# Memory rows by DMA, a shorter keep-warm block and another order of the first seven tiles in an attention, SoLU and top-1 MoE kernel

## Chip, cores and metric

The kernel runs on one core of a Trainium2 chip. The metric is device time in microseconds of the whole program, start to end. Lower is better.

## What is computed

Three layers follow each other on 3,072 tokens (4 batches of 768) with 512 features. Cut to what matters:

```python
# attention: 8 heads of 64, chunks of 32 queries; each sees 8 memory keys and the keys 16 before to 8 after its chunk
for c in range(24):
    k_full = concat([mem_k, k[:, :, max(0, 32*c - 16):min(768, 32*c + 40)]])
    v_full = concat([mem_v, v[:, :, max(0, 32*c - 16):min(768, 32*c + 40)]])
    out[:, :, 32*c:32*c + 32] = softmax(q_c @ k_full.T / 8) @ v_full
x = out as (3072, 512)
# SoLU layer, 512 -> 1024 -> 512
h = x @ w_in
s = h * softmax(h)
x = ((s - mean(s)) / sqrt(var(s) + 1e-6) * g_ln) @ w_out
# top-1 mixture of 8 experts, 512 -> 1024 -> 512
e = argmax(x @ w_gate)
out = softmax(x @ w_gate)[e] * sigmoid((x @ w_output_gate)[e]) * (relu(x @ w1[e]) @ w2[e])
```

`w_in`, `w_out` and `g_ln` reach the program as 64-bit floats (w_in and w_out in 32-bit halves); a float32 is made of each value on VectorE.

## The kernel before

The tokens are cut into 24 tiles of 128. Each tile goes through attention (scores, row maximum, exponentials, normalisation, transpose, product with v), then through the SoLU layer (first product, its row maximum, exponentials, squares, normalisation, transpose by DMA, second product) and the routing. After that the experts run over gathered rows. Products with the layers' weights are done in float16 in three passes, with a high and a low half of each operand.

Every step of a tile is registered with `at(t, fn)`, where t is a time of a schedule. At the end the steps are sorted by t and emitted in that order. So t only sets the order in which each engine's instructions, and the DMA issues on SyncE, stand in their queues; each queue runs in order and waits for data and for free buffers. From tile 7 on a tile has a fixed pattern with a period of 14.2 us of the schedule. The first seven tiles, all loads of that time and the conversion of the weights have their times written out by hand in the dictionary `PLAN`. `STEADY` is the place in that list that is set equal to five periods of the pattern: `when(name)` returns `PLAN[name] - STEADY + 5 * PERIOD`. In the list `w0` to `w3` load the four blocks of w_in and `w4` to `w7` those of w_out, and `b1`, `b2`, `b3`, `hi` and `lo` unpack them and make their halves. `k`, `q` and `v` load operands (k and q for two tiles each, v for one), `win` and `mkc` build the keys of a tile from its k and the memory keys, `sc` to `xlo` are the attention, `pin` and `hm` to `lt` the SoLU layer, `po` and `x2` its second product, `lg` to `rk` the routing.

`VW[0]` and `VW[1]` are two buffers with the values of two tiles each: eight chunks of 32 queries, on partitions 8 to 63 and 72 to 127 the 56 rows of v, on partitions 0 to 7 and 64 to 71 the eight memory rows, repeated for each chunk. For the first two pairs of tiles `first_mv` loads the memory rows once (two DMAs of 8 KB), and `copy_mv` repeats them into the buffers, by ScalarE for `VW[0]` and by VectorE for `VW[1]`. Later pairs use `load_mv`, in which a DMA reads the rows once for each chunk. The weight blocks have four buffers for eight loads, q and k two each; a load that takes a buffer again waits on SyncE for its last reader.

`WARM` lists blocks of matmuls on a constant tile, each of 384 columns, whose result nothing reads. An entry is its time in the list, the number of matmuls and the PSUM tile they write. The first block stands ahead of all other work of TensorE.

## Time and profile before

| | |
|---|---|
| median of 3 runs | 636.5 us (636.02 to 636.7) |
| the profiled execution | 635.88 us, span from first to last instruction 634.2 us |
| granted TensorE clock, mean of the span | 0.995 |
| TensorE matmul busy | 611.4 us (96%) |
| VectorE busy | 407.1 us (64%) |
| ScalarE busy | 311.1 us (49%) |
| GpSimd busy | 175.9 us (28%) |

The profile is of one execution. Busy time is a union of an engine's instructions and says nothing on which of them others wait for; keep-warm matmuls count as busy. Times in rows are microseconds from the span's start. The operations on w_in and w_out appear under the tile names `wd` (as loaded), `da` (as unpacked), `win_hl` and `wout_hl` (their halves).

### The profile page before, as it was taken

To read this page: it belongs to the slowest core of one execution; us is meant where nothing else is said; L and a number is where in the kernel's file an instruction comes from. 1 tells how busy PE (TensorE), PEld (TensorE's weight loads), DVE (VectorE), ACT (ScalarE), POOL (GpSimd) and SP (SyncE) were. 2 spreads that over 40 slices of the span, in tenths; PEclk is the share of its full clock that TensorE was granted. 3 is DMA by queue.
4 is the path that set the end of the run, shared out by engine and by line. 5 is a ranking of instruction groups with operands and counts; after the bars stand their busy time and mean duration, and the time that the engine had idled before them with its cause. 6 is when DMAs were issued, how large, how long until landed. Compare 5 with 4: busy or idle time off the path is not lost.

```text
span 634.2 us, 17086 instructions
## 1 busy us (share of the span) xinstructions
PE 611.4 (96%) x6955; PEld 338.3 (53%) x6955; DVE 407.1 (64%) x1209; ACT 311.1 (49%) x648; POOL 175.9 (28%) x201
## 2 busy tenths in 40 slices
PE   9999899999999999999999999999999999999993
PEld 5555445555555545545554455554554656657561
DVE  3999865878888788887876674566062537365020
ACT  5677864555665556645444242464152526444120
POOL 2213342334322343323333016030121312313101
PEclk9999999999999999999999999999999999999998
DMA  8985879699999999986459368997566485793101
GB/s 262 344 259 117 182 181 175 163 181 206 259 204 219 197 204 221 199 157 123 101 109 196 89 189 246 245 337 239 192 169 224 93 315 157 252 215 99 37 8 41
DMA packets 168262, 117.44 MB, mean 185 GB/s; under 512 B 125724, under 2 KB 149678, under 8 KB 167664
## 3 DMA queue, kind: packets, MB, share of 16 engines
q1 hardware_dynamic: 162096, 96.94, 66.1%
q0 software_dynamic: 6080, 19.34, 9.7%
q8 instruction: 56, 0.92, 0.7%
q14 instruction: 30, 0.25, 0.1%
HBM read 73.69 MB, written 12.94 MB: 137 GB/s over the span
## 4 chain that ended last, share of the span: by engine, by line
PE 37%; issue 25%; DVE 18%; POOL 6%; ACT 6%; DMA 4%; SPq 2%; POOLq 0%; ACTq 0%; DVEq 0%
PE h L582 11%; PE pt L350 8%; PE pg L350 5%; PE pt L1276 5%; DMA out_dram<-eh,split 3%; POOL out_dram L1334 3%; PE warm L909 3%; DVE nm L592 2%; ACT eh L600 2%; POOL xg L1238 2%; PE sc L367 2%; DVE eh L604 2%; DVE mx L381 1%; PE xo L458 1%; DVE e L385 1%
## 5 line engine op out<-in xcount | busy, mean ns | idle before, releaser
L582 PE MATMUL h<-win_hl,xT 128*128 128x512 f16 x576 | 131.7, 379 | 2.9 <-DVE eh L604 1.4
L350 PE MATMUL pt<-wout_hl,lnT 128*128 128x512 f16 x552 | 129.2, 379 | 1.2 <-DVE x L186 1.1
L1276 PEld LDWEIGHTS <-ru 128*128 128x128 f16 (+2 forms) x1176 | 70.1, 100 | 63.7 <-issue 5.6
L1262 DVE SCALAR_TENSOR_TENSOR ru<-pg,ru 128x320 f16<-128x320 f32 (+5 forms) x72 | 37.6, 525 | 102.6 <-ACT ru L1261 102.2
L582 PEld LDWEIGHTS <-xT 128*128 128x128 f16 x576 | 53.1, 98 | 63.7 <-issue 2.5
L350 PEld LDWEIGHTS <-lnT 128*128 128x128 f16 x576 | 53.2, 97 | 57.4 <-issue 1.5
L350 PE MATMUL pg<-xu,hl 128*128 128x320 f16 (+2 forms) x480 | 73.4, 312 | 0.7 <-ACT junk L621 0.6
L1261 ACT ACTIVATE ru<-pg 128x320 f16<-128x320 f32 (+5 forms) x72 | 33.5, 466 | 81.9 <-PE pg L350 80.0
L1276 PE MATMUL pt<-hl,ru 128*128 128x512 f16 (+2 forms) x528 | 72.8, 321 | 0.0
L648 POOL TENSOR_TENSOR lnhl<-eh,lnhl 128x1024 f16<-128x1024 f32 x23 | 49.5, 2152 | 77.7 <-ACT lnhl L644 64.6
L1276 PE MATMUL pt<-wout_hl,ru 128*32 128x128 f16 (+2 forms) x648 | 60.7, 285 | 1.2 <-issue 0.9
L350 PE MATMUL pg<-xu,win_hl 128*128 128x480 f16 (+3 forms) x384 | 59.5, 316 | 0.0
L350 PEld LDWEIGHTS <-hl 128*128 128x128 f16 x480 | 46.1, 98 | 25.0 <-DMA xu<-xg 0.7
L1334 POOL DMA_INDIRECT out_dram<-eh,slots_sidx x17 | 17.5, 1027 | 146.4 <-ACT eh L1333 146.4
L350 PEld LDWEIGHTS <-win_hl 128*128 128x128 f16 x384 | 37.2, 98 | 21.5 <-issue 0.8
L600 ACT ACTIVATE eh<-h,nm 128x1024 f32<-128x1024 f32 x24 | 26.8, 1115 | 41.8 <-DVE zr L793 34.8
L419 POOL TENSOR_TENSOR e<-e,sm 128x512 f32<-128x512 f32 x24 | 28.7, 1197 | 62.1 <-DVE sm L416 45.0
L186 DVE SCALAR_TENSOR_TENSOR hl<-wf,hl 128x1024 f16<-128x1024 f32 x32 | 38.7, 1224 | 11.0 <-ACT hl L1225 10.5
L1225 ACT ACTIVATE hl<-wf 128x1024 f16<-128x1024 f32 x32 | 32.9, 1047 | 4.2 <-DMA wf<-in_moe_w_dram 4.2
L604 DVE SCALAR_TENSOR_TENSOR eh<-h,eh 128x1024 f32<-128x1024 f32 x24 | 29.4, 1223 | 6.3 <-ACT eh L600 6.3
L909 PE MATMUL warm<-wide 128*128 128x384 f16 x169 | 31.6, 346 | 1.4 <-DVE mhalf L156 1.4
L621 ACT ACTIVATE junk<-eh,su 128x1024 f16<-128x1024 f32 x24 | 27.7, 1153 | 8.7 <-DVE pr L616 6.9
(193 smaller groups left out, 833.2 us busy)
## 6 DMA issues: line engine op xcount, KB each, us to landing
wf<-in_moe_w_dram SPq DMA_DIRECT2D x14, 2048.0 KB
vw<-in_v_dram SPq DMA_DIRECT2D x96, 112.0 KB
kr<-in_k_dram SPq DMA_DIRECT2D x12, 560.0 KB
qt<-in_q_dram SPq DMA_DIRECT2D x12, 512.0 KB
x2d<-x POOLq DMA_DIRECT2D x23, 260.0 KB
wd<-in_moe_w_in_dram SPq DMA_DIRECT2D x4, 1024.0 KB
wd<-in_moe_w_out_dram SPq DMA_DIRECT2D x4, 1024.0 KB
wf<-in_moe_w_dram SPq DMA_DIRECT2D x8, 512.0 KB
```

What stands on the lines that cost most here:

```text
L186: nc.vector.scalar_tensor_tensor(out=lo, in0=src, scalar=s, in1=hi, op0=ALU.mult, op1=ALU.subtract)
L350: nc.tensor.matmul(out=out_ap, lhsT=a, rhs=b_, start=(z == 0), stop=(z == n - 1))
L582: nc.tensor.matmul(out=v["h"][:, n * HALF:(n + 1) * HALF], lhsT=xt[:, a * KD + kk], rhs=win_hl[:, b_, kk, n * HALF:(n + 1) * HALF], start= ...
L600: nc.scalar.activation(out=v["e"], in_=v["h"], func=AF.Exp, bias=v["nm"], scale=IH, accum_out=v["se"])
L604: nc.vector.scalar_tensor_tensor(out=e, in0=v["h"], scalar=IH, in1=e, op0=ALU.mult, op1=ALU.mult, accum_out=v["su"])
L648: eng.tensor_tensor(out=v["ln"][:, 1], in0=v["e"], in1=v["ln"][:, 0], op=ALU.subtract)
L909: nc.tensor.matmul(out=t[:, 0:3 * P], lhsT=wide[:, 0:P], rhs=wide, start=True, stop=True)
L1225: nc.scalar.activation(out=hl[b, m][:, 0, cs], in_=wf[m if of is None else of][:, cs], func=AF.Copy, scale=(S_W1, S_W2)[m])
L1261: nc.scalar.activation(out=r[:, 0, f, 0:cap(n)], in_=ps, func=AF.Relu)
L1262: nc.vector.scalar_tensor_tensor(out=r[:, 1, f, 0:cap(n)], in0=ps, scalar=0.0, in1=r[:, 0, f, 0:cap(n)], op0=ALU.max, op1=ALU.subtract)
L1276: nc.tensor.matmul(out=y_t[n, piece][q * m:(q + 1) * m, 0:DM // fold], lhsT=r[:, a, kk, at_:at_ + m], rhs=wt[:, b_, kk, q * DM // fold:(q ...
L1334: put = nc.gpsimd.indirect_dma_start(out=out if fold == 1 else out.rearrange("n (h d) -> (n h) d", h=fold), out_offset=bass.IndirectOffset ...
```

## The change

The memory rows of `VW[0]` and `VW[1]` come through `load_mv`, two DMAs for each buffer, and the small tile `mvs` with its load and its copies goes. `PLAN` has other times throughout, and with them another order; `STEADY` goes from 93.08 to 90.52. The keep-warm blocks go from 9 with 169 matmuls together to 12 with 126, the first of them from 68 to 40. The gate weights (`gates`) are loaded early rather than late, g (`g`) later, and w_in's first block comes first of all. Code outside of this list and of the memory rows stays. The list has new names `fa0` to `fa4` that no code reads.

```diff
     VW = [ap_.tile([P, UC, GD], F32, name=f"vw{n}", bufs=1) for n in range(2)]
-    mvs = f64.tile([P, GD], F32, name="mvs", bufs=1)
...
-    def first_mv():
-        for j in range(2):
-            nc.sync.dma_start(out=mvs[64 * j:64 * j + M], in_=mv[0, j])
-
-    def copy_mv(u):
-
-        for j in range(2):
-            out, in_ = VW[u][64 * j:64 * j + M], mvs[64 * j:64 * j + M].unsqueeze(1).to_broadcast([M, UC, GD])
-            if u == 0:
-                nc.scalar.activation(out=out, in_=in_, func=AF.Copy)
-            else:
-                nc.vector.tensor_copy(out, in_)
...
     PLAN = {
-        "mvs": 0.8, "k0": 1.6, "w0": 2.1, "mk": 2.6, "q0": 3.1, "cmv1": 4.5, "cmv0": 4.5, "g": 4.8, "w1": 6.49,
-        "v0": 6.99, "win1": 8.3, "w2": 8.69, "w3": 9.19, "win0": 9.27, "b1_0": 9.6, "mkc0": 10.24, "k2": 10.36,
-        "b2_0": 10.39, "mkc1": 11.55, "k1": 11.62, "b3_0": 11.7, "sc0": 12.05, "prep_g": 12.85, "w7": 12.97,
-        "hi_0": 12.97, "rmax0": 13.05, "q1": 13.47, "mkc2": 13.75, "mkc3": 13.9, "shift0": 14.05, "lo_0": 14.15,
-        "exp0": 14.2, "b1_1": 15.29, "b2_1": 16.05, "sc1": 16.67, "gr0": 17.21, "b3_1": 17.48, "mkc4": 18.63,
-        "hi_1": 18.75, "nrm0": 18.78, "rmax1": 18.78, "lo_1": 19.83, "tr0": 19.94, "ev0": 20.69, "b1_2": 20.97,
-        "v1": 21.34, "att0": 21.41, "mkc5": 21.61, "shift1": 21.76, "b2_2": 21.86, "exp1": 21.91, "b3_2": 23.12,
-        "xhi0": 24.26, "b1_3": 24.27, "win4": 24.81, "gr1": 24.91, "b2_3": 25.18, "win5": 25.78, "b3_3": 26.44,
-        "hi_2": 26.75, "xlo0": 27.59, "nrm1": 27.59, "hi_3": 27.71, "xt0": 28.33, "pin0_0": 28.33, "lo_2": 28.63,
-        "win2": 28.67, "win3": 29.64, "lo_3": 29.77, "pin0_1": 30.49, "b1_7": 30.91, "b2_7": 31.67, "pin0_2": 31.78,
-        "pin0_x": 32.22, "b3_7": 32.93, "pin0_3": 33.08, "sc2": 33.51, "hm0": 34.08, "hi_7": 34.2, "w5": 34.3,
...
+        "w0": 0.8, "k0": 1.3, "q0": 1.8, "mk": 2.25, "w1": 2.75, "k1": 3.25, "mv0": 3.75, "w2": 4.65, "v0": 5.15,
+        "b1_0": 6.5, "gates": 6.85, "b2_0": 7.26, "win1": 8.4, "b3_0": 8.52, "q1": 8.85, "v1": 9.3, "win0": 9.37,
+        "hi_0": 10.34, "mkc1": 10.45, "mkc3": 10.6, "mkc0": 10.75, "mkc2": 10.9, "w3": 11.0, "sc0": 11.02,
+        "lo_0": 11.42, "w7": 11.5, "k2": 12.0, "v2": 12.5, "rmax0": 12.56, "b1_1": 13.26, "shift0": 13.9,
+        "b2_1": 14.02, "exp0": 14.05, "g": 14.2, "b3_1": 15.28, "mv1": 15.56, "win2": 16.4, "gr0": 16.52,
+        "sc1": 16.52, "w5": 16.55, "nrm0": 16.94, "win3": 17.37, "q2": 17.52, "rmax1": 17.52, "tr0": 18.1,
+        "mkc4": 18.14, "shift1": 18.29, "hi_1": 18.34, "mkc5": 18.39, "b1_2": 18.54, "b2_2": 19.3, "ev0": 19.3,
+        "exp1": 19.9, "att0": 20.02, "lo_1": 20.46, "v3": 21.47, "b3_2": 21.6, "sg_hi": 22.25, "sc2": 22.37,
+        "xhi0": 22.55, "prep_gate": 22.75, "hi_2": 23.1, "gr1": 23.1, "rmax2": 23.4, "nrm1": 23.52, "xlo0": 24.02,
+        "lo_2": 24.64, "xt0": 24.76, "tr1": 24.76, "pin0_0": 25.31, "ev1": 25.51, "shift2": 25.78, "b1_3": 26.0,
+        "exp2": 26.11, "b2_3": 26.76, "att1": 27.47, "b3_3": 28.02, "sc3": 28.58, "v4": 28.75, "xhi1": 28.75,
+        "b1_7": 29.17, "hi_3": 29.3, "pin0_1": 29.38, "xlo1": 29.81, "win4": 30.4, "gr2": 30.43, "xt1": 30.55,
+        "pin0_2": 30.68, "lo_3": 30.73, "pin0_x": 31.11, "win5": 31.37, "b2_7": 31.87, "pin0_3": 31.99,
+        "nrm2": 33.03, "hm0": 33.03, "tr2": 34.19, "prep_g": 34.28, "mkc6": 34.4, "he0": 34.4, "b3_7": 34.55,
...
-        "pk1": 93.08, "x2l2": 94.23, "pe1": 94.35, "p21": 94.85, "x2t2": 94.97, "pz1": 95.0,
+        "x2l2": 89.85, "lg1": 90.01, "xhi6": 90.21, "pk1": 90.52, "x2t2": 91.18, "xlo6": 91.67, "pe1": 91.79,
...
-    STEADY = 93.08
+    STEADY = 90.52
...
-    WARM = ((1.45, 68, 0), (12.9, 21, 0), (17.52, 13, 0), (20.54, 3, 0), (22.54, 33, 0), (34.91, 5, 0), (37.2, 13, 0), (48.93, 10, 0), (58.64, 3, 0))
+    WARM = ((1.45, 40, 0), (11.87, 26, 0), (17.37, 2, 0), (18.7, 6, 0), (21.15, 5, 0), (23.22, 7, 0), (32.47, 8, 0), (34.79, 7, 0), (43.67, 7, 0), (45.84, 3, 0), (54.5, 3, 0), (56.5, 12, 0))
...
-    at(when("mvs"), first_mv)
+    for n in range(2):
+        at(when(f"mv{n}"), load_mv, n)
     at(when("mk"), load_mk)
...
-    for n in range(2):
-        at(when(f"cmv{n}"), copy_mv, n)
```

Further back in the list, w_out's blocks are loaded at 16.55 (`w5`, before 34.3), 42.93 (`w4`, before 35.79) and 43.43 (`w6`, before 48.77).

## Rows read from the trace of the kernel before

**Rows 1.** Busy time by stretch: busy us (instructions) by engine, clock, DMA share, GB/s.

```profile
core 0: us, PE busy (x) PEld busy (x) DVE busy (x) ACT busy (x) POOL busy (x), PEclk, DMA share, GB/s
0.00:7.50 7.50, 6.12 (x22) 3.03 (x23) 2.82 (x4) 6.39 (x6) 4.40 (x22) 1.00 0.63 220
0.00:10.00 10.00, 8.62 (x38) 4.52 (x39) 4.45 (x7) 7.08 (x7) 4.40 (x22) 1.00 0.78 240
10.00:20.00 10.00, 9.56 (x125) 5.67 (x130) 5.56 (x12) 3.52 (x17) 0.00 (x0) 1.00 1.03 346
20.00:30.00 10.00, 9.74 (x178) 6.47 (x179) 9.86 (x17) 6.45 (x25) 3.15 (x2) 1.00 1.08 332
...
60.00:62.00 2.00, 2.00 (x130) 1.80 (x131) 1.91 (x3) 0.05 (x1) 0.63 (x1) 1.00 0.96 167
90.50:91.50 1.00, 0.40 (x2) 0.19 (x2) 1.00 (x9) 0.69 (x3) 0.00 (x0) 1.00 0.35 101
...
100.00:110.00 10.00, 9.97 (x166) 5.13 (x167) 6.68 (x27) 4.29 (x9) 1.64 (x2) 1.00 0.99 193
```

**Rows 2.** Busy time by stretch, for the parts of the opening.

```profile
1.39:6.48 5.09, 5.09 (x17) 2.38 (x18) 2.44 (x2) 4.78 (x4) 3.69 (x16) 1.00 0.75 249
6.48:15.18 8.70, 8.70 (x61) 5.12 (x66) 3.31 (x6) 2.76 (x5) 0.00 (x0) 1.00 1.10 313
8.37:37.53 29.16, 27.41 (x371) 16.07 (x372) 24.51 (x37) 13.93 (x47) 3.69 (x2) 1.00 1.06 332
37.53:98.19 60.66, 56.27 (x929) 31.54 (x920) 50.18 (x127) 44.70 (x144) 21.77 (x16) 1.00 0.73 170
```

**Rows 3.** TensorE's order of time: start, length, operation, idle before.

```profile
1.39 13.79 PE L909 MATMUL warm<-wide 128*128 128x384 f16 x68 [1.39 <-DVE mhalf L156]
15.11 0.86 PE L367 MATMUL sc<-kt,qt 64*32 64x64 f32 x64
15.90 3.59 PE L909 MATMUL warm<-wide 128*128 128x384 f16 x21
```

**Rows 4.** VectorE's order of time in the opening.

```profile
2.37 2.47 DVE L314 COPY vw<-mvs 8x2048 f32<-8x2048 f32 x2 [1.04 <-DMA mvs<-in_mem_v_dram]
8.37 0.69 DVE L222 TENSOR_SCALAR da<-wd 128x1024 int32<-128x1024 int32 x1 [3.53 <-DMA wd<-in_moe_w_in_dram]
...
16.06 0.17 DVE L377 MEMSET sc<- 32x128 f32 x1 [4.37 <-PE sc L367]
...
37.53 1.22 DVE L592 TENSOR_REDUCE nm<-h 128x1 f32<-128x1024 f32 x1
```

**Rows 5.** VectorE's groups between 8.37 and 37.53: busy us, mean ns, idle before.

```profile
L232 DVE SCALAR_TENSOR_TENSOR da<-wd,da 128x1024 int32<-128x1024 int32 x5 | 6.8, 1356 | 0.1
...
L381 DVE TENSOR_REDUCE mx<-sc 128x8 f32<-128x512 f32 x2 | 1.4, 684 | 0.0
...
L186 DVE SCALAR_TENSOR_TENSOR xT<-xo,xT 128x512 f16<-128x512 f32 x1 | 0.7, 678 | 0.0
...
L377 DVE MEMSET sc<- 32x128 f32 x1 | 0.2, 165 | 4.4 <-PE sc L367 4.4
L257 DVE TENSOR_SCALAR g_sc<-g_sb 128x8 f32<-128x8 f32 x1 | 0.2, 160 | 0.0
```

**Rows 6.** DMA issues on the page: count, KB each.

```profile
vw<-in_v_dram SPq DMA_DIRECT2D x96, 112.0 KB
kr<-in_k_dram SPq DMA_DIRECT2D x12, 560.0 KB
qt<-in_q_dram SPq DMA_DIRECT2D x12, 512.0 KB
...
wd<-in_moe_w_in_dram SPq DMA_DIRECT2D x4, 1024.0 KB
```

**Rows 7.** TensorE's groups between 1.4 and 98.2, seven tiles each.

```profile
L447 PE MATMUL xo<-aT,vw 64*64 64x32 f32 x448 | 7.9, 220 | 0.5 <-ACT aT L433 0.5
L367 PE MATMUL sc<-kt,qt 64*32 64x64 f32 x448 | 6.0, 224 | 1.6 <-ACT e L403 1.0 <-ACT kt L327 0.5
```

**Rows 8.** TensorE's order of time, one of the later first products.

```profile
67.09 5.34 PE L582 MATMUL h<-win_hl,xT 128*128 128x512 f16 x24 [1.40 <-DVE eh L604]
```

54 rows, old and new, of the table PLAN are left out of this document.

## Prediction

> **What bounds the kernel now.** I read four views of the profile in this order. The busy time by stretch comes first. From 100 us on TensorE is busy 9.97 us in 10 at a granted clock of 1.00 [rows 1], so whatever ends the opening of the kernel earlier passes whole into the end. The opening itself lasts until TensorE begins tile 5's first product at 98.19 us, since everything up to there follows the hand-written list that the change rewrites. In it TensorE looks busy too, but much of that is keep-warm work. The engine that carries the opening is VectorE: 24.51 us busy between 8.37 and 37.53, 50.18 of the 60.66 us after that [rows 2].
>
> The second view is TensorE's order of time. The opening keep-warm block of 68 matmuls runs from 1.39 and the first scores start at 15.11, right behind it with no wait of their own [rows 3]. The block, not the data, sets their time. The reader is also to see its pace: 17 instructions in the 5.09 us to 6.48, about 0.30 us each, then 51 matmuls until 15.11, which is 0.17 us each [rows 2, 3]. The clock column says 1.00 in both stretches, but 384 columns in 0.17 us is the pace of the 2.4 GHz level and 0.30 us is near that of 1.2 GHz.
>
> The third is VectorE's order of time. It waits 3.53 us for the first block of w_in, starts unpacking at 8.37, and then stands still for 4.37 us until 16.06, for the scores behind that block [rows 4]. From there to the row maximum of tile 0's hidden layer at 37.53 it has practically no hole: the groups of that stretch show 4.4 us of waiting for scores and 0.1 us besides on the groups shown [rows 5]. So 37.53 = 8.37 + 24.51 of work + 4.65 of standing.
>
> The fourth is the DMA columns. The queues move 346 and 332 GB/s at a share of 1.03 and 1.08 [rows 1]: between 10 and 30 us they are full, and an operand's time is its place in the order of bytes.
>
> **The change part by part.** The profiled execution took 635.88 us with a span of 634.2, so 1.7 us lie around the span, and it is 0.62 under the median of 636.5. The sum below is a difference, taken off the median. All times of "after" are estimates from the named rows.
>
> *Opening block, 68 to 40 matmuls.* The 28 that go are at the fast end: 28 x 0.17 = 4.7 us [rows 3]. The first scores can start at 15.11 - 4.7 = 10.4. They need k, q and the memory keys of the first two tiles: with w_in's first block 2.2 MB, the same bytes that before reached the chip in front of everything else. By the byte rates 2.4 MB are moved by 10.0 [rows 1]; without the two small loads in front they end up to 0.8 us earlier, so the data is there at about 9.7 and the memory-key copies at about 10.2. The block and the data end together.
>
> *Copies out, DMA in.* The two VectorE copies (2.47 us) lay in the wait for w_in [rows 4], and ScalarE's lay beside them. Removing them is worth nothing by itself. What takes their place is 2 x 64 KiB for each of two buffers, by the code's shapes: 0.13 MB each time into 16 of 128 partitions. The row that shows such a load nearly alone is 90.50 to 91.50, where 101 GB/s went at a share of 0.35 [rows 1]. At that rate one pair takes 1.3 us; at the full rate of 346 GB/s it delays the queue by 0.4 us. I take 0.8 for the first pair. The second comes behind the loads that matter here. The Trainium skill (DMA: Bandwidth & Descriptors, section on why a DMA increments its semaphore by 16) says that a transfer runs on as many engines, up to 16, as divide its slowest dimension, so 8 rows use 8 engines. The share of 0.35 agrees with half or fewer; by that rule the other eight go on, the delay is nearer 0.6 us than 1.3, and the sum would be 0.2 us better.
>
> *Order of loads.* w_in's first block is now the first transfer. Before, the 0.57 MB of k lay ahead of it [rows 6]. 1.65 MB had moved by 7.5 [rows 1], which is k and this block, and unpacking began 0.9 us later. Without k's bytes it is 1.3 us (at 0.43 MB/us) to 1.7 us (at 0.346) earlier, and 0 to 0.8 us more because nothing is issued in front. I take 2.1 of the 1.3 to 2.5: **unpacking starts at 6.3 instead of 8.37.**
>
> The gate weights move from 59 us into the full stretch: 0.03 MB in 32-byte pieces. The row of 60 to 62 us, where they move, shows 167 GB/s instead of 346 at a share of 0.96 [rows 1], so they cost 0.1 to 1.0 us. The g vector (1,024 pieces of 4 bytes) leaves the front of that stretch and gives part of it back. Net I take 0.3. w_in's last block is the one that is now late. It has 7.55 MB in the queue up to and with it: four blocks of 1.05, two k of 0.57, two q of 0.52, two v of 0.46 (four pieces of 0.115 each), 0.23 of memory rows, keys and gates [rows 6]. 5.86 MB move by 20 us, the rest at 332 GB/s takes 5.1, and 0.9 is added as above: 26.0. With 0.4 us off for the earlier start, and 0.8 and 0.3 on, it is there at 26.7, bounds 25.3 to 28.0.
>
> *VectorE's first stretch.* The new list puts before tile 0's row maximum the same unpacking, splitting and memory-key copies, less one last unpack step (1.36) and the scaling of g (0.16), and more by one score maximum (0.68), one shift, guard and reciprocal (0.5), one low half of x (0.68) and the gates' low half (some 0.2) [rows 5]. That is +0.6: 25.1 us. The holes are these. After the first block's three steps and four copies (3.9 us, to 10.2) its low half waits for ScalarE, 0.8. Of the last block, VectorE asks for it at about 26.5 (19.4 us of the work stand before it) and gets it at 26.7, 0.2 in the middle and 1.5 at the bound. Score maxima and exponentials of tiles 1 and 2, each 0.2 to 0.5: 1.1 together. Holes 2.1, bounds 0.8 to 4.5. Row maximum: 6.3 + 25.1 + 2.1 = **33.5 against 37.53, a gain of 4.0**, bounds 0.9 to 5.8.
>
> *From there to tile 5.* The work moved ahead leaves this stretch: 0.6 us on VectorE, and on TensorE two tiles' scores and one tile's attention, 2 x 0.86 + 1.13 = 2.8 us [rows 7], while the keep-warm matmuls behind it stay about as many (31 and 32). TensorE is busy 56.27 of 60.66 us here [rows 2]. If only VectorE's part counts the gain is 0.6, if TensorE's does 2.8, and new collisions between engines can take 1.0. I take 0.9, near the lower end, since most waits here end on VectorE.
>
> *Covers.* The later loads of w_out (two blocks at 43 in the list) have no reader before 49, in a stretch with room on the queue. The wait for a free buffer that the fifth weight load makes on SyncE holds k, v and q of later tiles behind it, but its buffer comes free at 9.5, before SyncE asks. The memory rows now written by DMA have their reader, the attention of tile 0, at about 20; they stand ahead of v in the queue, so v is what lands last.
>
> Sum: 4.0 + 0.9 = 4.9 us; 636.5 - 4.9 = **631.6 us**. A check by another way: in the trace before, the first scores ran at 15.11 where the list had 12.05, and tile 5's product about 5.2 later than listed, so 2.2 us were lost after the scores. The new list's end is 2.56 earlier and its scores lose nothing; with the same 2.2 lost the gain is 5.2 - 2.2 + 2.56 = 5.6, and less with the late w_in block.
>
> **The rivals.**
>
> *Loads late.* The queue carries more ahead of w_in's last block than I priced: narrow loads at 101 GB/s and 32-byte pieces at 167. If both come at their upper bounds, VectorE stands 1.5 us at this block and some 0.5 at w_out's first one, and all behind moves. 631.6 + 2.0 = 633.6. For it speaks the DMA share above 1; against it that everything before that block lands ahead of need.
>
> *The clock falls once.* With fewer keep-warm matmuls TensorE may stand idle after the opening block if the scores are late. A new climb is 17 instructions at 0.30 instead of 0.17, 2.2 us [rows 2], on the way to tile 1's scores: 633.8. Against it: an idle of 1.40 us before a product at 67.09 left that product at 5.34 us for 24 matmuls, 0.22 each, the fast level [rows 8]. The Trainium skill (TensorE: Matmul & The Clock Gate, Part 1) has the clock follow recent activity, which is why a fall is possible at all; the row bears out that a short gap is harmless.
>
> *The other side: tiles 0 and 1's first products run at the low level.* Before, 33 keep-warm matmuls led up to tile 0's product; now 5 and 7 stand among small attention matmuls. At 1.2 GHz a product of 24 takes 5.3 us more [rows 8]. One such product cancels the gain (637), two give 636.5 - 4.9 + 10.6 = 642.2; it decides from 22 slow product matmuls on. Against it stand the same rows as above.
>
> *Nothing reaches the end.* If another chain held tile 5's product, the end would stay at 636.5. VectorE has 15 us free of the 89.8 and could not hold it alone; the transposes and transfers of late tiles could. Only the dense TensorE from 100 us on speaks against it.
>
> **How the numbers follow.** About 0.2%, 1.3 us, is what a measurement can tell from no change. Forecast (629.4 to 632.9): 0.60. Loads late (to 634.0): 0.17. One fall of the clock (to 634.6): 0.08. More than forecast: 0.02. Nothing reaches the end: 0.07. Slow products: 0.06. Faster 0.87, same 0.07, slower 0.06. The range 629.4 to 634.6 takes in the bounds of the first stretch's holes and of the second stretch, and leaves out less than 2 in 10.
>
> **What would show it.** First unpack step at 6 to 7 us; first scores at 10.4 to 11, released by the block or the memory-key copies; no hole over 1.5 us on VectorE before tile 0's row maximum, and that at 32.5 to 34.5; tile 5's product at 92 to 95. It would be wrong if VectorE waits over 2 us for w_in's last block, if keep-warm matmuls after 10 us run at 0.3 us, or if tile 5's product comes at 92 to 95 and the span does not shrink with it.

## The result

The changed kernel took 641.48 us in the median of 19 runs, the kernel before 636.84 in 19 runs beside them: a ratio of 1.006, 95% interval 1.0041 to 1.0078 (taken without the slowest execution of after; it is not the quotient of the two medians). Forecast were 631.6 us (629.4 to 634.6) and a chance of 0.06 for slower; **the forecast was wrong in its sign.** The profiled execution of after took 635.91 us (span 634.1), the fastest of its 19; it shows where the opening lost its gain, and the median is 5.6 us longer. These 5.6 us go with TensorE's clock: the two executions at a mean granted clock of 0.993 took 635.91 and 636.37 us, the two at 0.982 took 642.86 and 644.04, and the median of the 19 clocks is 0.988. The kernel before had 0.995 in its profile and 0.994 or 0.995 in the medians of all later groups.

The busy time by stretch of after comes first (columns as in [rows 1]):

```profile
0.00:10.00 10.00, 8.13 (x40) 4.35 (x41) 4.12 (x9) 3.56 (x6) 2.53 (x22) 1.00 0.84 292
10.00:20.00 10.00, 8.20 (x168) 5.07 (x168) 7.27 (x15) 6.99 (x29) 1.04 (x1) 1.00 1.07 267
6.09:35.95 29.86, 24.36 (x486) 14.71 (x484) 25.10 (x41) 19.46 (x71) 3.91 (x3) 1.00 1.03 284
35.95:98.35 62.40, 56.90 (x767) 30.41 (x766) 49.51 (x123) 41.71 (x125) 20.71 (x15) 0.97 0.79 195
```

From 10 to 20 us the queues move 267 GB/s where before moved 346 [rows 1], at a share that is no lower. The first stretch of VectorE has 25.10 us of work, as forecast, and 4.76 us of holes (29.86 less 25.10) where 2.1 were priced. The second is 1.74 us longer than before [rows 2], and its clock is below 1.

VectorE's order of time of after has the holes; it answers to [rows 4]:

```profile
6.09 0.70 DVE L222 TENSOR_SCALAR da<-wd 128x1024 int32<-128x1024 int32 x1 [4.75 <-DMA wd<-in_moe_w_in_dram]
...
19.36 0.69 DVE L222 TENSOR_SCALAR da<-wd 128x1024 int32<-128x1024 int32 x1 [1.24 <-DMA wd<-in_moe_w_in_dram]
...
28.22 0.69 DVE L222 TENSOR_SCALAR da<-wd 128x1024 int32<-128x1024 int32 x1 [1.29 <-DMA wd<-in_moe_w_in_dram]
...
35.95 1.22 DVE L579 TENSOR_REDUCE nm<-h 128x1 f32<-128x1024 f32 x1
```

The third and the fourth block of w_in are late, at 19.36 and 28.22. The third was issued at 6.08 and was in the queue until 19.33. Why the fourth was late, SyncE's order of time tells, and below it what SyncE waited for in its first 22 us (in total, times, longest):

```profile
6.08 0.36 SPq L201 DMA_DIRECT2D wd<-in_moe_w_in_dram  x1
7.71 4.54 SPq L293 DMA_DIRECT2D vw<-in_v_dram  x4
14.77 0.40 SPq L250 DMA_DIRECT2D wg<-in_moe_w_gate_dram  x1
...
19.35 1.92 SPq L293 DMA_DIRECT2D vw<-in_v_dram  x4
21.52 0.36 SPq L201 DMA_DIRECT2D wd<-in_moe_w_in_dram  x1
```

```profile
SPq L293 <- DMA wd<-in_moe_w_in_dram: 5.0, 2, 3.1
SPq L250 <- DMA kr<-in_k_dram: 2.5, 1, 2.5
SPq L201 <- DMA vw<-in_v_dram: 0.2, 1, 0.2
```

The last block, listed at 11.0, is issued at 21.52, behind gates, q1 and v1, which themselves went out late. The forecast had put it in a queue of bytes; it was not in the queue. The trace has the rule behind this. SyncE's loads take eight semaphores in turn, and an issue waits until the load eight issues before it has landed: the 9th goes out at 6.08 when the 1st has landed (6.06), the 14th (gates) at 14.77 when the 6th has (14.75), the 17th (v1) at 19.35 when the 9th has (19.33), and the 21st, w_in's last block, at 21.52 when the 13th, a piece of v0, has (21.50). None of these waits is for a buffer. Each load takes one of the eight places whatever its size: v0 takes four, the memory rows and the gates two each.

TensorE's order of time of after [rows 3] shows the rest (rows between those shown are left out):

```profile
1.39 8.13 PE L895 MATMUL warm<-wide 128*128 128x384 f16 x40 [1.39 <-DVE mhalf L156]
10.01 0.85 PE L353 MATMUL sc<-kt,qt 64*32 64x64 f32 x64 [0.50 <-DVE kt L316]
29.64 0.74 PE L353 MATMUL sc<-kt,qt 64*32 64x64 f32 x51
32.44 0.34 PE L353 MATMUL sc<-kt,qt 64*32 64x64 f32 x13 [2.06 <-issue]
79.87 4.04 PE L336 MATMUL pt<-wout_hl,lnT 128*128 128x512 f16 x18 [1.36 <-DVE x L186]
89.52 5.73 PE L336 MATMUL pt<-wout_hl,lnT 128*128 128x512 f16 x18 [2.41 <-DVE x L186]
98.35 2.32 PE L569 MATMUL h<-win_hl,xT 128*128 128x512 f16 x10
```

Three readings. The scores start at 10.01, 5.1 us earlier. In the scores of tile 3 TensorE stops for 2.06 us after 51 of 64 matmuls with no releaser ("issue"). And behind the idle of 2.41 us at 89.52 the same 18 matmuls take 5.73 us that took 4.04 at 79.87; the granted clock from 89.5 to 95.5 us was 0.72, so part of this stretch ran at 1.2 GHz instead of 2.4. The kernel before waited 1.11 us in the same place:

```profile
91.11 2.75 PE L350 MATMUL pt<-wout_hl,lnT 128*128 128x512 f16 x12 [1.11 <-DVE x L186]
```

Tile 5's product comes at 98.35, not before the 98.19 of [rows 2].

### The profile page after: what moved, and what is told of

The parts are those of the page before. It is cut to its first block, busy times and chain, and to the rows that moved or that the text cites. A ratio compares the mean times of both kernels' runs of the same rounds, so it can differ in the third digit from the quotient of the medians.

```text
span 634.1 us, 16991 instructions
## 1 busy us (share of the span) xinstructions
PE 606.2 (96%) x6912; PEld 334.7 (53%) x6912; DVE 406.1 (64%) x1207; ACT 307.6 (49%) x646; POOL 173.7 (27%) x201
## 4 chain that ended last, share of the span: by engine, by line
issue 26%; PE 25%; DVE 21%; DMA 11%; ACT 7%; POOL 6%; SPq 1%; POOLq 0%; ACTq 0%; DVEq 0%
PE pt L336 7%; PE h L569 7%; PE pg L336 5%; DMA out_dram<-eh,split 3%; POOL out_dram L1320 3%; DVE nm L579 3%; DMA wd<-in_moe_w_in_dram 2%; POOL xg L1224 2%; DVE eh L591 2%; DMA vw<-in_v_dram 2%; ACT eh L587 2%; PE pt L1262 2%; DVE mx L367 1%; DVE x L186 1%; DVE e L371 1%
## 5 line engine op out<-in xcount | busy, mean ns | idle before, releaser
L336 PE MATMUL pt<-wout_hl,lnT 128*128 128x512 f16 x552 | 130.9, 383 | 4.0 <-DVE x L186 3.8
L1247 ACT ACTIVATE ru<-pg 128x320 f16<-128x320 f32 (+5 forms) x72 | 33.5, 467 | 83.8 <-PE pg L336 81.1
L405 POOL TENSOR_TENSOR e<-e,sm 128x512 f32<-128x512 f32 x24 | 26.6, 1107 | 58.2 <-DVE sm L402 28.5
L620 POOL TENSOR_TENSOR rt<-vr,mhalf 128x1 f32<-128x1 f32 x24 | 14.4, 602 | 70.6 <-DVE vr L616 70.5
L608 ACT ACTIVATE junk<-eh,su 128x1024 f16<-128x1024 f32 x24 | 27.6, 1152 | 10.4 <-DVE pr L603 9.8
```

The lines of the kernel that those rows point to most:

```text
L336: nc.tensor.matmul(out=out_ap, lhsT=a, rhs=b_, start=(z == 0), stop=(z == n - 1))
L608: nc.scalar.activation(out=junk, in_=v["e"], func=AF.Square, bias=v["su"], scale=1.0, accum_out=v["sq"])
L1247: nc.scalar.activation(out=r[:, 0, f, 0:cap(n)], in_=ps, func=AF.Relu)
```

## The experiments

18 kernels ran, in five groups (the first letter of the name), each group on one chip beside the kernel before. Ratios are to the kernel before on the same chip, with 95% intervals, so kernels of different groups are compared through it; the last column is the median over the timed executions of their mean granted clock (before: 0.994 or 0.995 in each group).

| kernel | what it is | ratio | interval | clock |
|---|---|---|---|---|
| a1_again | the changed kernel | 1.0071 | 1.0046 to 1.0096 | 0.986 |
| a2_copies | after, memory rows loaded and copied as before | 1.0038 | 1.0017 to 1.0059 | 0.989 |
| b1_rows_dma | before, memory rows by DMA | 0.9989 | 0.9971 to 1.0006 | 0.994 |
| b2_block40 | before, opening block 40 | 1.0009 | 0.9989 to 1.0030 | 0.990 |
| c1_x2h1 | after, high half of x2 earlier on ScalarE | 1.0000 | 0.9973 to 1.0027 | 0.991 |
| c2_sc3 | after, tile 3's scores later | 1.0015 | 0.9986 to 1.0043 | 0.991 |
| c3_three | a2, c1 and c2 together | 0.9971 | 0.9950 to 0.9992 | 0.992 |
| c4_block54 | before, opening block 54 | 0.9955 | 0.9936 to 0.9974 | 0.995 |
| d1_after_padded | after, 43 tiny matmuls more | 1.0035 | 1.0015 to 1.0056 | 0.987 |
| d2_before_padded | before, short block, 68 matmuls in it | 0.9958 | 0.9938 to 0.9978 | 0.993 |
| d3_before_fewer | before, 30 keep-warm matmuls fewer, same time | 1.0030 | 1.0007 to 1.0052 | 0.994 |
| d4_gates_late | after, gates loaded late | 1.0067 | 1.0041 to 1.0092 | 0.986 |
| e1_order | after, opening block 68 | 1.0103 | 1.0069 to 1.0137 | 0.986 |
| e2_block54p | after, opening block 54, padded | 1.0109 | 1.0077 to 1.0140 | 0.987 |
| e3_x2h1_pad | c1, padded | 1.0029 | 1.0008 to 1.0050 | 0.990 |
| e4_three_pad | c3, padded | 0.9983 | 0.9966 to 1.0001 | 0.993 |
| f1_order_rows | e1 with 51 wider keep-warm matmuls for 68 | 1.0103 | 1.0080 to 1.0127 | 0.988 |
| f2_after_rows | after with 30 wider ones for 40 | 1.0045 | 1.0022 to 1.0068 | 0.988 |

**The parts alone.** a1 is the changed kernel, unedited. b1, b2 and c4 put one part into the old order; a2 takes one out of the new.

```
b1: "mvs": 0.8 ... "cmv1": 4.5, "cmv0": 4.5   ->  "mv0": 6.95, "mv1": 43.35   (load_mv as in the change)
b2: WARM (1.45, 68, 0) -> (1.45, 40, 0)        c4: -> (1.45, 54, 0)
a2: "mv0": 3.75, "mv1": 15.56  ->  "mvs": 0.7, "cmv1": 4.5, "cmv0": 4.5
e1: WARM of after, (1.45, 40, 0) -> (1.45, 68, 0)
```

> The changed kernel once more, to see another execution. Theory C (TensorE's clock falls in most executions, a few us each, where TensorE stands idle behind late operands in the opening): 640 to 643 us, mean granted clock 0.983 to 0.989, and the clock below 1.00 in two or more stretches of the first 100 us, each some 3.4 us long and behind an idle of TensorE over 2 us. Theory L (loads alone: the queue is slower in some executions, the clock plays no part): 640 to 643 us with the clock at 1.00 in all stretches up to 100 us and the extra time in waits on DMA.

> The changed kernel with the memory rows as before: two loads of 8 KB in front and the four copies on ScalarE and VectorE. If the narrow row loads starve the DMA queue (L), the stretch 13 to 15 us moves over 250 GB/s instead of 159 and 117, tile 0's first row maximum comes at 34 to 34.5 instead of 35.95, and the median falls by 2 to 5 us to 636.5 to 639. If the rows don't matter and the clock falls for other reasons (the list alone), the median stays within 1.5 us of the changed kernel's 641.5.

> The kernel before with the memory rows by DMA alone, ahead of v of tile 0 and of tile 2. If the narrow loads starve the queue, the second and third blocks of w_in land 1 to 2 us later, but its opening has that much slack ahead of them: 636.5 to 638. If they are harmless: 636.8 within 0.6.

> The kernel before with the opening keep-warm block cut from 68 to 40 and nothing else. By the prediction's reading the first scores come at 10.4 instead of 15.11 and VectorE's standing of 4.4 us goes: up to 4 us faster, 633 to 634. If the rest of the opening is paced by loads instead, gain under 1.5 us. If the shorter block lets the clock fall, slower than 636.8 with a mean clock under 0.992.

> The kernel before with the opening block at 54, halfway. The opening should end 2.0 us earlier (first product of tile 5 at 96.2). With 40 it ended 4.0 us earlier, but the span was only 1.3 us shorter, because TensorE stood idle 2.5 us at 388 us, where expert 1's rows come through DRAM, and the clock fell there. If that wait is systematic, here too some 1 to 2 us of idle show at 386 to 392 and the median is within 0.6 us of before. If it was one execution's chance, the median falls by 1.5 to 2 us.

> The changed kernel with the opening block of the kernel before, 68 matmuls: of the change only the narrow loads, the new order and the later keep-warm blocks are left (15 matmuls fewer in all). First theory (the gaps come from the new list: the low half of x2 behind a wait on ScalarE, scores of tile 3 set early, v late): first scores at 14.8 to 15.2, tile 0's row maximum at 37.5 to 39, the gap of 2.4 us before the output product near 90 to 93 is there all the same, and the kernel is slower than before, ratio 1.003 to 1.008. Rival (the short opening block is what makes TensorE run into late operands; with the long one all operands are there): no gap over 1.2 us before 100 us, ratio 0.996 to 1.001.

The narrow loads cost nothing measurable in the old order (b1). In the new one they stand in front of the third block of w_in: from 13 to 15 us after moves 138 GB/s and a2 429, and a2's last block is unpacked at 27.40 instead of 28.22; its row maximum comes at 35.73, a gain of 0.2 us only, and the interval of its ratio overlaps that of a1. The block of 40 in the old order (b2) brings tile 0's row maximum to 33.34, 4.2 us earlier, and tile 5's product to 94.16, 4.0 earlier; the ratio is 1.0009 all the same, and where that went is told below. With 54 (c4) scores start at 12.85, row maximum and tile 5's product come 2.3 and 1.8 us earlier, and this gain is kept: 0.9955, one of the two fastest kernels of the study.

e1 answers the main question. With the old long opening block the new order is not better but worse, 1.0103: so the short block is not what made the change slow. Its scores start at 14.93 (before 15.11), and tile 0's row maximum comes at 41.91 against 37.53. The hole, in TensorE's order of time of e1:

```profile
26.04 0.71 PE L353 MATMUL sc<-kt,qt 64*32 64x64 f32 x46 [0.16 <-ACT e L389]
30.25 0.63 PE L353 MATMUL sc<-kt,qt 64*32 64x64 f32 x18 [3.51 <-issue]
```

**What TensorE stops for in the middle of scores.** Counted over TensorE's order of time, the stop in after comes behind the 475th matmul of its program, the one in e1 behind the 349th (rows 962 and 707 in the expectations, which count the weight loads too): some 255 instructions apart. I took these for the ends of blocks in which the program is fetched. The word "issue" alone does not say so: c1 and d1 also stop under that word, for 1.66 and 0.64 us, at the first matmul of tile 0's attention, the 207th of c1 and, with the 43 matmuls more of d1, its 250th; those two stops stay with the matmul and not with the count, and no packet of the program ended in the 3 us before their end. In the DMA queues of e1 between 26.75 and 30.25, in which TensorE is busy 0.00 us, there is this besides data:

```profile
q1 hardware_dynamic: 487, 1.34, 98.3%
q8 instruction: 1, 0.02, 2.0%
```

One packet of the instruction queue, with the 16 engines busy with data 98% of the time. Four kernels move the row without touching the scores or their operands.

```
e2: WARM (1.45, 54, 0), and behind it 29 matmuls of 64 columns: 15 matmuls more than e1
e3: opening block 27 of 384 columns and 56 of 64: 43 matmuls more than after
f1: 51 matmuls of 512 columns for the 68 of e1: 17 fewer
f2: 30 matmuls of 512 columns for the 40 of after: 10 fewer
```

> The changed kernel with an opening block of 54 matmuls of 384 columns, and 29 tiny ones of 64 columns so that its program is as long as the one before. First theory (gaps of the new list): first scores at about 13.5, row maximum of tile 0 at 36 to 37 since w_in's last block still comes at 28, the 2.4 us gap near 90 stays, ratio 1.002 to 1.005. Rival (block too short): TensorE no longer meets late operands, ratio 0.994 to 0.998, as the kernel before with 54.

> The new order with the long opening block, but that block as 51 matmuls of 512 columns instead of 68 of 384: the same time, 34 weight loads and matmuls fewer ahead of everything else. With 68, TensorE stood 3.51 us inside tile 2's scores, after 46 of their 64 matmuls, at its row 707. Theory (TensorE stops where a block of 256 rows of its program ends, because the next one is not yet fetched): row 707 now lies behind tile 2's scores, which run whole; the stop of 1 to 3.5 us, if TensorE is still ahead of the fetch, stands in the keep-warm matmuls behind them or at row 450 or 962, and tile 0's row maximum comes at 38.5 to 41 instead of 41.91; ratio 1.005 to 1.009. Rival (these 64 matmuls wait for data of their own, k, q or the memory keys): the stop of about 3.5 us stays after 46 of 64, row maximum at 41.5 to 42.5, ratio 1.010.

> The changed kernel with its opening block as 30 matmuls of 512 columns instead of 40 of 384: the same time, 20 rows fewer. In the changed kernel TensorE stood 2.06 us inside tile 3's scores, after 51 of 64, at row 962. Theory (end of a block of the program): row 962 now lies 7 rows behind these scores, so they run whole, and the stop stands in tile 0's second product part that follows, after 3 or 4 of its 14 matmuls, or is gone. Rival (data of the scores): it stays after 51 of 64. The time stays as in the changed kernel, ratio 1.004 to 1.008, in either case: the same stop ahead of the same product.

Each pair of lines is TensorE's order of time of one kernel: e2, f1, f2, e3.

```profile
25.29 0.45 PE L353 MATMUL sc<-kt,qt 64*32 64x64 f32 x31 [0.16 <-ACT e L389]
29.77 0.63 PE L353 MATMUL sc<-kt,qt 64*32 64x64 f32 x33 [4.03 <-issue]
```

```profile
26.10 0.84 PE L353 MATMUL sc<-kt,qt 64*32 64x64 f32 x63 [0.21 <-ACT e L389]
30.45 0.24 PE L353 MATMUL sc<-kt,qt 64*32 64x64 f32 x1 [3.50 <-issue]
```

```profile
29.53 0.82 PE L353 MATMUL sc<-kt,qt 64*32 64x64 f32 x61
32.44 0.30 PE L353 MATMUL sc<-kt,qt 64*32 64x64 f32 x3 [2.08 <-issue]
```

```profile
31.04 0.32 PE L353 MATMUL sc<-kt,qt 64*32 64x64 f32 x8
33.27 0.78 PE L353 MATMUL sc<-kt,qt 64*32 64x64 f32 x56 [1.91 <-issue]
```

In tile 2's scores the stop moved from 46 of 64 to 31 with 15 matmuls more and to 63 with 17 fewer; in tile 3's from 51 to 8 with 43 more and to 61 with 10 fewer. It moves one for one with the count, always behind the 349th and the 475th matmul (e1, e2, f1; after, f2, e3). If the scores waited for data of their own, the rival, the stop would stay at the same matmul. The trace has the other end of it too: in each of these six kernels a packet of 16 KB on the instruction queue is under way, and the stop ends 1.2 to 1.5 us after it (in after the packet takes 29.83 to 30.98 and the stop ends at 32.44, in e1 27.74 to 28.85 and 30.25). The expectations of f1 and f2 had the end of the block behind the last score; they were short by one and by three matmuls, so the stop stayed in the scores, and the times as they were. e2 as a whole came to 1.0109, no better than e1. Before has the same ends of blocks, but its 349th matmul lies in tile 0's first product, behind 33 keep-warm matmuls; they run from 25.25 to 30.79, and the packet (26.83 to 27.97) falls among them.

The Trainium skill (Runtime: NRT & Kernel Launch, section Instruction fetch mechanics) says that the program comes in blocks of 16 KiB, 256 instructions, and that crossing into the next is mostly hidden. The distance of the stops agrees; the cost does not: 0.78 to 4.03 us in the first 40 us here, and the measurement decides for this stretch, in which the DMA engines are full.

**The two repairs of the list, and both with a2.**

```
c1: "x2h1": 81.73 -> 81.7     (ScalarE: ahead of tile 8's key windows)
c2: "sc3": 28.58 -> 32.46
c3: both, and a2
```

> The changed kernel with one exchange on ScalarE: the high half of tile 1's second-layer input (x2h1) ahead of the key windows of tile 8 instead of behind them. In the three traces of the new list TensorE stands idle 2.41 us behind this step, and the clock falls there for 3.4 or 6.8 us each time. Theory C (these falls are the price): the idle at 89.5 becomes 1.4 to 1.5 us, no stretch below 1.00 follows it, and the median of the timed runs falls by 2 to 3.5 us against the changed kernel's own distance to the kernel before (from +0.7% and +0.5% to +0.1 to +0.3%). Theory L (late loads alone): 0.9 us at the most.

> The changed kernel with tile 3's scores moved behind tile 0's whole first product. In all three traces of the new list TensorE stops for 1.8 to 2.2 us inside those scores at the same instruction (the 962nd or 963rd of its matmuls and weight loads) without waiting for any engine, 2 to 2.6 us after an instruction block began to be fetched. If the dense run of 256 small instructions (tile 1's attention, then tile 3's scores) outruns the fetch, the stop goes or falls under 0.5 us, as 28 slower instructions now stand there; tile 0's row maximum comes at 34.5 to 35.3 instead of 35.95, and the time falls by 0.5 to 1.5 us. If the stop is a wait for an operand of tile 3's scores, it moves along with them.

> The changed kernel with the memory rows as before, tile 3's scores behind tile 0's product, and x2h1 ahead of the windows. If the three losses add (narrow loads 1.1 us, fetch stop 1, falls of the clock 2 to 3), it ends 0 to 1 us under the kernel before and its mean clock is back at 0.993 or more. If the list itself is worse paced than the old one, it stays 1 us or more over it.

The idle of 2.41 us at 89.52 ends on VectorE's low half of x2 for tile 1, which itself waited 0.95 us for ScalarE's high half (L654). ScalarE's order of time, of after and then of c1:

```profile
86.09 1.15 ACT L608 ACTIVATE junk<-eh,su 128x1024 f16<-128x1024 f32 x1 [1.00 <-DVE pr L603]
...
87.23 0.61 ACT L312 ACTIVATE kt<-kr 128x512 f32<-128x512 f32 x1
87.75 0.51 ACT L313 ACTIVATE kt<-kr 128x384 f32<-128x384 f32 x1
88.17 0.57 ACT L654 ACTIVATE x<-pt 128x512 f16<-128x512 f32 x1
```

```profile
90.28 1.15 ACT L608 ACTIVATE junk<-eh,su 128x1024 f16<-128x1024 f32 x1 [1.00 <-DVE pr L603]
...
91.43 0.57 ACT L654 ACTIVATE x<-pt 128x512 f16<-128x512 f32 x1
91.91 0.62 ACT L312 ACTIVATE kt<-kr 128x512 f32<-128x512 f32 x1
```

One step of the list changes places with two copies that nobody waits for, and TensorE's idle falls to 1.48 us; the product behind it takes 4.05 us, as at the full clock. The ratio falls from 1.0071 (a1) to 1.0000. That is 4.5 us for a wait that became 0.93 shorter; most of the rest goes with the clock, whose median rises from 0.986 to 0.991, an estimated 3.2 us of 635 (0.005 of the time). c2 takes the stop out of tile 3's scores (TensorE then stands 1.60 us for w_in's last block instead) and gives 1.0015, at a clock of 0.991 too; but its row maximum comes at 36.83, later than in after and not earlier as expected, so its gain does not lie there. All three together, 0.9971, beat the kernel before: against a1 that is 1.0%, more than the change had lost. They do not beat c4, whose interval overlaps theirs.

Over all 20 profiles the clock and the idle before it go together in part. Each kernel has an idle of 1.35 to 1.40 us before a product between 63 and 86 us, and in none did the clock fall there. Ten have the idle of 2.41 or 2.42 us at the place above; the clock fell in it or right behind it in eight and not in c2 and d1. Four have 1.48 us there; it fell in e4 and not in c1, c3 and e3. In c1's profile it fell at 22.0 and 35.7 instead, behind two stops of 1.66 and 1.60 us.

**Gates.**

```
d4: "gates": 6.85 -> 50.9, "sg_hi": 22.25 -> 63.3, "prep_gate": 22.75 -> 69.3
```

> The changed kernel with the gate weights (32-byte pieces) loaded at 50.9 in the list instead of 6.85, and their two steps of preparation at 63.3 and 69.3. Theory of late loads: the stretch from 13 to 15 us moves over 250 GB/s instead of 159 and 117, v of tile 0 lands 0.8 to 1.0 us earlier, w_in's last block is unpacked from 27.2 to 27.6 instead of 28.2, tile 0's row maximum comes at 34.8 to 35.4 instead of 35.95; the end gains under 1 us, since the later gaps and falls of the clock stay: ratio 1.004 to 1.006. Rival (the 32-byte pieces do not hold the queue; the narrow memory rows or the eight transfers under way do): rates and times as in the changed kernel, ratio 1.006 to 1.007.

The rival holds: from 13 to 15 us d4 moves 122 GB/s and after 138, the last block is unpacked at 28.65, and the ratio is 1.0067. The 32-byte pieces were not what held the queue; by a2, which takes the narrow memory rows out and moves 429 GB/s there, it was these rows.

**Where the gain of a shorter opening goes at 390 us.** In b2 TensorE stands 2.50 us at 388.05 for the rows of expert 1. They are gathered by GpSimd after the last store of x2, which SyncE issues behind a load of 2 MB. After, d3 and d1, first the store, then the gather, then TensorE's product with these rows:

```
d1: after, opening block 27 of 384 columns and 56 of 64: rows behind it as in the kernel before
d2: before, opening block 27 of 384 columns and 41 of 64: short, and as many matmuls as 68
d3: before, blocks 68, 21, 33 of 384 columns -> 51, 16, 25 of 512: same time, 60 rows fewer
```

> The changed kernel with 43 matmuls more on TensorE, all of them tiny: the opening block is 27 keep-warm matmuls of 384 columns and 56 of 64 columns, so that it takes about as long as 40 but TensorE's program has as many instructions behind the block as the kernel before. Theory (a 16 KB instruction fetch in the store's window makes expert 1's rows 1.1 us late): the gather of these rows starts 4.7 to 5.0 us after the last store of x2 is issued instead of 5.9 to 6.1, TensorE's idle of about 1.0 us near 390 is gone, the stop inside tile 3's scores at 32 us is gone or stands elsewhere, and the time falls by 1.0 to 2.0 us, to a ratio of 1.003 to 1.005 to the kernel before. Rival (the place of the fetches does not matter, late loads and the clock are all): gather at 5.9 to 6.1, idle of 0.9 to 1.1 stays, ratio 1.006 to 1.007 as in the changed kernel.

> The kernel before with an opening block as short as 40 matmuls but with 68 instructions pairs in it: 27 of 384 columns and 41 of 64 columns. Theory: first scores at 10.5 to 11.0, tile 5's first product 3.5 to 4.1 us earlier than before, the gather of expert 1's rows 4.7 to 5.0 us after the store, no idle at 388, and the gain stays: ratio 0.994 (0.993 to 0.996), about 630.6 us. Rival (the short block itself brings the later idle and the fall of the clock, wherever the fetches lie): the gain of the opening is given back near 388 as with 40 matmuls of 384 columns, ratio 0.999 to 1.002.

> The kernel before with 30 keep-warm matmuls fewer in the same time: the blocks of 68, 21 and 33 matmuls of 384 columns become 51, 16 and 25 of 512 columns. Theory: the opening is as before (first scores at 15.1, tile 5's first product at 97 to 98.5), but a fetch comes into the store's window, the gather of expert 1's rows starts 5.8 to 6.1 us after the store instead of 4.7, TensorE stands idle 1.0 to 2.5 us near 390, and the kernel is slower: ratio 1.002 to 1.005. Rival (place of the fetches does not matter): no idle at 390, ratio 1.000 within 0.001.

```profile
372.93 0.36 SPq L776 DMA_DIRECT2D x2d<-x  x1
378.80 1.02 POOL L1224 DMA_INDIRECT xg<-x2d,slots_gidx  x1 [10.31 <-DMA x2d<-x]
390.44 7.77 PE L336 MATMUL pg<-xu,hl 128*128 128x320 f16 x56 [1.09 <-DMA xu<-x]
```

```profile
375.18 0.36 SPq L789 DMA_DIRECT2D x2d<-x  x1
381.01 1.02 POOL L1239 DMA_INDIRECT xg<-x2d,slots_gidx  x1 [10.17 <-DMA x2d<-x]
394.18 4.10 PE L350 MATMUL pg<-xu,hl 128*128 128x320 f16 x29 [2.57 <-DMA xu<-x]
```

```profile
373.58 0.36 SPq L776 DMA_DIRECT2D x2d<-x  x1
378.18 1.02 POOL L1226 DMA_INDIRECT xg<-x2d,slots_gidx  x1 [9.08 <-DMA x2d<-x]
390.35 7.90 PE L336 MATMUL pg<-xu,hl 128*128 128x320 f16 x57 [0.34 <-DMA xu<-x]
```

From store to gather after takes 5.87 us, d3 5.83, b2 6.07; the kernel before takes 4.67 and d1 4.60. The packets of the instruction queue go with it, over all 20 profiles: eleven have one between store and gather, which then takes 5.81 to 6.10 us, and nine have none and take 3.54 to 5.30 (3.54 is d2, whose gather VectorE released and not the store). What such a packet does is seen in the rate of the queues in slices of 0.15 us from the store on, of after and then of d1:

```profile
GB/s 382 411 437 437 437 410 410 437 437 492 382 410 382 382 410 410 410 382 437 255 169 65 28 29 27 27 27 27 27 1 1 0 0 0 0 0 0 0 0 0
GB/s 412 411 383 437 382 410 437 437 437 437 382 437 437 437 410 437 382 437 437 203 40 3 0 0 0 0 0 0 0 0 0 0 0 109 0 0 0 0 0 0
```

After has a tail of seven slices, 1.05 us, at 27 to 29 GB/s, about a sixteenth of the rate before: one of the 16 engines is left with work. The packet itself took 1.01 us. d1 has no such tail. So each keep-warm matmul taken out early moves the ends of all later blocks, and in some kernels a fetch falls among the packets of the load whose end the store waits behind. TensorE's idle near 390 is 0.80 to 3.17 us in the eleven, and under 0.7 us in the nine but for e1, which has 2.15 without a packet.

What this costs is less sure than that it happens. d3 has the opening of before (scores at 15.27) and is slower, 1.0030, at the same clock of 0.994; but the 2.57 us at 394 are not its only loss: its profile has two more stops with no releaser, 0.50 us at 43.26 and 1.46 us at 181.96, and tile 5's product comes at 99.00, 0.8 later than before. d2 has the short block and is faster, 0.9958, where b2, as short, had 1.0009, and these intervals lie apart; but its profiled execution has stops of 1.21 and 1.59 us in the first 40 us and tile 5's product at 97.33, so the gain that it keeps is not the 3.5 to 4.1 us that were expected there. In the old order, then, the number of matmuls in the same time changes the kernel's time; the share of the gather at 390 is not measured by itself. In the new order not even the first is shown: d1 is 0.36% below a1 with intervals that overlap, and the two runs meant to confirm it did not.

> The changed kernel with two edits: the step that makes the high half of x2 for tile 1 set 0.03 earlier in the list (it then stands ahead of tile 8's key windows on ScalarE), and the opening block of 27 matmuls of 384 columns and 56 tiny ones. If the two causes add up as they did alone (0.71% and 0.36% off 1.0071), the ratio is 0.9965 (0.994 to 0.998), the gap near 90 is 1.3 to 1.6 us, and no idle stands near 390. Rival (the gain of the one contains the other, since both act by the clock): ratio 0.999 to 1.000.

> All four repairs of the changed kernel: memory rows loaded once and copied, tile 3's scores later in the list, the high half of x2 for tile 1 earlier, and the opening block of 27 matmuls of 384 columns with 56 tiny ones. It has no idle near 390 and no stop in tile 3's scores. If the place of the fetches counts for 1.0 to 2.0 us here as in the changed kernel, ratio 0.9945 (0.993 to 0.996), about 630.5 us, the fastest of all. Rival (it is worth nothing once the other gaps are closed): ratio 0.997 as without the tiny matmuls.

e3, c1 padded, came to 1.0029 instead of 0.9965, and e4, c3 padded, to 0.9983 instead of 0.9945. Both have the early gather (4.80 and 4.70 us), and e4 has no idle over 0.6 us near 390; but e3 has its stop behind the 475th matmul again, and one of 1.54 us behind the 222nd, in tile 1's scores. The same padding that takes a fetch away from the gather puts another into the scores: in e3 the repairs do not add up, since each moves the ends of blocks for all that follows. e4 has no stop with no releaser over 0.4 us before 270 us and is no faster than c3 (0.9971) all the same; its rival holds, and where its expected gain went is not shown.

## Why the prediction was wrong

Two steps failed, of about equal weight. The opening gained nothing: tile 5's product was forecast 4.9 us earlier and came 0.16 later (98.35 for 98.19), so 5.1 us were lost even in the fastest execution, 1.7 of them by the one fall of the clock in it. And the clock falls more than once in most executions (17 of 19 have a mean clock below the 0.993 of that one): the sum had no term for it, and the rival that named it had a chance of 0.08. The median clock is 0.988 instead of 0.995, an estimated 4.5 us of 636 (0.007 of the time). The distance from 631.6 to 641.48 is 9.9. Without the falls of the clock the change would have been worth between nothing and 2 us, by estimate: the median less these 4.5 us is 637.0, and the line through the clocks and times of its executions gives 635.0 at 0.995. With them it is slower. That the clock makes the time, and not the other way round, is argued from c1, which shortens one idle: the clock rises and the time falls.

- **Opening block.** Scores at 10.4 forecast, 10.01 measured; first unpack 6.3 and 6.09. Right. The block alone, in the old order, was worth the 4.0 us that the forecast gave to the whole first stretch (b2), or 2.3 with 54 (c4).
- **Order of loads.** w_in's last block was forecast at 26.7 with a bound of 28.0, and came at 28.22. The term for the narrow loads, 0.8, was right: without them the block came 0.82 earlier (a2). The 0.3 for gates was about right in being small (d4). What was missing altogether is SyncE: the load went out at 21.52, when the eighth load before it had landed, and shared the queue with loads that had been counted behind it. By 28.2 us the queues had moved about 8 MB (the rows above, and 302 GB/s from 20 us on), where 7.55 were to be enough. The third block, of which the forecast said that all before the last lands ahead of need, made VectorE wait 1.24 us as well.
- **VectorE's first stretch.** This is the step that failed first in time. The work was right (25.10 for 25.1), the holes were 4.76 against 2.1, beyond the bound of 4.5: 2.53 of them for the two blocks, 0.64 for ScalarE, 0.9 for scores. The row maximum came at 35.95 instead of 33.5. The program's fetch had no place in the sum at all: in after its stop lies beside VectorE's work, and the clock did not fall there; in e1 VectorE waits 3.7 us for the scores in which TensorE stands, most of the 4.4 us by which its row maximum is later than before's.
- **Second stretch.** Forecast a gain of 0.9, measured a loss of 1.74. "New collisions can take 1.0" was the right thought and too cheap: 2.41 us of idle where the kernel before had 1.11, 1.36 us before tile 0's product where it had none, and 1.7 us of a product at the low clock.
- **Passing to the end.** "Whatever ends the opening earlier passes whole into the end" was false: b2 had 4 us in hand at 94 us and gave them back at 388 and behind it. TensorE busy 9.97 of 10 us from 100 to 110 [rows 1] says nothing of 390.
- **The rivals.** "The clock falls once" had the right mechanism at a chance of 0.08 and a price of 2.2 us once. The idle of 1.40 us in [rows 8], after which the pace was the fast one, was taken as proof for idle of any length; behind 2.41 us it did not hold. The price is in the median: a1 runs at a mean clock of 0.986, before at 0.995. The Trainium skill (TensorE: Matmul & The Clock Gate, Part 1) has the clock follow how busy TensorE has been of late; these rows agree with that. "Slow first products" named another place than the one where it happened. "Loads late" was right in kind, 2.53 us of waiting for two blocks where it had 1.5 for one, and too cheap by itself. The three signs of being wrong did not help: VectorE waited 1.29 us for the last block and not over 2, the keep-warm matmuls after 10 us ran at 0.17, and tile 5's product did not come at 92 to 95.

What stays open: how the 6.6 us of e1 (1.03% of 636.25) divide between the stop in tile 2's scores (3.5 us), the late half of x2 and the clock, since these act on each other; which of the idles makes the clock fall in a given execution (behind 2.41 us the granted clock was 0.72 in after and 0.78 in f2, but 1.00 in d1); and whether any list with this order would be faster than c4. The nearest, e4, with its block ends in harmless places as far as its profile shows, came to 0.9983.

## What to carry to other kernels

Keep-warm matmuls, which are there for the clock, do something else that a table of busy times does not show: they give the next block of the program time to arrive. Whoever removes them or reorders small matmuls should ask where the ends of its blocks, some 250 instructions apart, will then fall, and whether the DMA engines are full there. An operand's time starts when its load can be issued, here when the eighth load before it has landed; its place in a sum of bytes is not enough. A gap of 2.4 us on TensorE can cost more than itself, since the clock may fall behind it, and one profiled execution need not show that price. A gain in an opening is to be followed through every later meeting of a DMA chain with TensorE before it is added to the end; here 54 keep-warm matmuls instead of 68, one number, gave 0.45%, where the whole new list with 40 lost 0.6%.

## What the runs showed of the hardware

TensorE stopped at the same three places of its program in kernels of either order: behind the 222nd matmul (0.78 us in d1, 1.60 in e2, 1.21 in d2), the 349th (3.51 in e1, 4.03 in e2, 3.50 in f1) and the 475th or 476th (2.06 in after, 1.91 in e3, 2.08 in f2, 1.59 in d2, 0.50 in d3), whatever matmul stood there: scores, attention, or in d2 a keep-warm one. Each stop ended 1.2 to 1.5 us after a packet of 16 KB on the instruction queue. And one such packet among the last of a 2 MB load went with rows gathered 1.2 us later, 350 us away from the edit that moved it: after's queues end with 1.05 us at a sixteenth of their rate.
